# Biased attention and two MoE layers on one core: two relus of sets 8 to 10 and a rounding of k go to ScalarE, and the bias rows are loaded in two pieces

## The chip, the cores and the metric

One core of a Trainium2 chip runs the whole program. The metric is device time in microseconds (us) of one execution. Lower is better.

## The reference, cut to what matters

```python
scores = scale * q @ k.T                                  # (2, 8, 576, 576), scale = 1/8
rel = pos[:, None] - pos[None, :]                         # pos = 0 .. 575
psi_rel, psi_i = log1p(abs(rel)), log1p(max(pos[:, None], 1))
x = (psi_rel / psi_i)[..., None]
h = maximum(x @ w1 + b1, 0)                               # 32 hidden values for each (i, j)
bias = h @ w2                                             # 8 heads
attn = softmax(scores + bias)                             # + 1e-9 in the denominator
y = attn @ v                                              # (2, 576, 8 * 64) -> 1152 tokens of 512
hh = y @ w_in;  y = (hh * clip(hh + 3, 0, 6) / 6) @ w_out  # 512 -> 2048 -> 512
y = ((y @ w_a) * (y @ w_b)) @ w_out2                      # 512 -> 1536 -> 512
```

Everything is float32. The numerator of x depends only on the distance of two positions, and its denominator only on the row, so the bias of row i is a function of the distance alone.

## The kernel before, in words

**Bias.** The 576 rows are worked in 36 *sets* of 16 (`bias_relu(s)`, L183, and `bias_mm(s)`, L196). A set has four `ht` tiles of 128 partitions (4 rows times 32 hidden values), one for each j of 0 to 3, with the distance along the free axis. Each tile takes one relu with a scale per partition. `RELU = "VVVA"` (L87) puts j = 0 to 2 on VectorE (L192) and j = 3 on ScalarE (L194). Four matmuls with w2 give 16 rows times 8 heads, and `bias_out` (L220) copies them out of PSUM into a tile `E`, mirrored for negative distances: ScalarE does the right side (L227), VectorE the mirrored left side (L229). Both add a constant from `cst3`, a column that holds 8 times the value of the relu at zero for the partitions whose relu is the VectorE form max(scale * x, -b1), which leaves b1 out. One DMA (L243) writes `E`, skewed, into a scratch tensor in DRAM, and eight sets fill one scratch of 128 rows.

**Loading the bias back.** `bias_load(it, half)` (L248) reads a scratch into a tile `bias` of 128 partitions and 4 heads. Even heads take one DMA (576 columns), odd heads two (512 and 64 columns, since odd heads are rotated by 64). Three buffers hold `bias` tiles.

**Attention.** 36 steps n (L452) of one pair of heads of 128 rows each. Step n does the scores of pair n (L299, three products of rounded parts `KH`, `KL`, `qh`, `ql`), the softmax of pair n (L310 on VectorE adds the bias and takes the extreme, L314 on ScalarE is the exponential), the normalisation (L329 on GpSimd), the transposes of pair n-1 and the product with v of pair n-2. Between them it makes the bias of set g = n + 10. So the scratch of rows 128 to 255 is complete with set 15, in step 5; it is first used in step 8. The next two are complete with sets 23 and 31, in steps 13 and 21, and are first used in steps 16 and 24.

**The order of work** is the order in which the code issues it, per engine; nothing reorders it. SyncE (SP) issues nearly all DMAs, in order, and an issue that waits holds up those behind it. Each DMA also takes one of eight completion counters in turn, so that it waits until the DMA eight places ahead has landed.

**Places that the change touches.** Sets 0 to 9 are worked ahead of step 0 (L417 to L437). After the mm of set 7 come, in the code: the load of k's part 4, the rounding of k's part 1 (`k_hi(1, A)`, L430), the relus of sets 8 and 9, the rounding of q (`q_hi(0)`), the rounding of k's part 0 (`k_hi(0, V)`, L434), and on VectorE the rests `k_lo(0)`, `q_lo(0)`, `k_lo(1)` (L170, L150). The relus of set 10 come ahead of step 0 (L449), then `k_work(-1)` with two more roundings on ScalarE and two rests on VectorE. In a step n with g = 15, 23 or 31, L499 and L500 load the first two pairs of heads of the finished scratch, after the write of set g has been issued.

**MoE.** After step 35 TensorE runs the two MoE layers (L567, L773) from weights that ScalarE, VectorE and GpSimd split into parts.

Of the kernel before, what the change touches and what calls it, by code (L numbers as in the profile page):

```python
# [19 lines left out]
PITCH = 640  # L20
# [30 lines left out]
def kernel(ctx, tc, cons, qm, qt, kt, vm, vt, wm, out):  # L51
# [32 lines left out]
    negb = ph.tile([128, 1], F32, name="negb")  # L84
    cst4 = ph.tile([128, 1], F32, name="cst4")
    cst3 = ph.tile([128, 1], F32, name="cst3")
    RELU = "VVVA"  # L87


    idle = ph.tile([128, S], F32, tag="h", bufs=8, name="idle")  # L90
# [13 lines left out]
    V.tensor_scalar(scl, rtab, scalar1=w1c, scalar2=None, op0=ALU.mult)  # L104
    V.tensor_scalar(negb, b1c, scalar1=-1.0, scalar2=None, op0=ALU.mult)
    V.memset(cst3, 0.0)
    make_identity(nc, ident)
    warm = ph.tile([128, 1], F32, name="warm")
    G.memset(warm, 0.0)
# [56 lines left out]
    def k_hi(j, eng):  # L166
        (A.copy if eng is A else eng.tensor_copy)(KH[:, j, :], kr[j])
# [15 lines left out]
    def bias_relu(s, only=range(4)):  # L183

        i0, R, Dd = bias_geom(s)
        if s not in h_tiles:
            h_tiles[s] = [ph.tile([128, S], F32, tag="h", bufs=8, name="ht") for _ in range(4)]
        for j in only:
            ht = h_tiles[s][j]
            sc = scl[:, 4 * s + j : 4 * s + j + 1]  # L190
            if RELU[j] == "V":
                V.tensor_scalar(ht[:, :Dd], ltab[:, :Dd], scalar1=sc, scalar2=negb, op0=ALU.mult, op1=ALU.max)  # L192
            else:
                A.activation(ht[:, :Dd], ltab[:, :Dd], AF.Relu, bias=b1c, scale=sc)  # L194
# [25 lines left out]
    def bias_out(s, rev, banks, cuts):  # L220

        i0, R, Dd = bias_geom(s)
        E = ph.tile([128, S + 16], F32, tag="E", bufs=4, name="E")

        def leave(eng, dst, src):
            if eng is A:
                A.activation(dst, src, AF.Identity, bias=cst3[:, 0:1], scale=8.0)  # L227
            else:
                V.tensor_scalar(dst, src, scalar1=8.0, scalar2=cst3[:, 0:1], op0=ALU.mult, op1=ALU.add)  # L229

        for bp, d0, d1 in zip(banks, cuts, cuts[1:]):
            f1 = min(d1, S - i0)
            few = rev is A and Dd > 512
            if f1 > d0:
                leave(V if few else A, E[:, R + d0 : R + f1], bp[:, : f1 - d0])
            r0, r1 = max(d0, 1), min(d1, R + 1)
            if r1 > r0:
                dst = E[:, R - r1 + 1 : R - r0 + 1]
                dst = bass.AP(dst.tensor, dst.offset + (r1 - r0 - 1), [dst.ap[0], [-1, r1 - r0]])
                leave(V if few and d0 else rev, dst, bp[:, r0 - d0 : r1 - d0])  # L240
        it, sl = divmod(s, 8)
        scr = scratch[it]
        SP.dma_start(  # L243
            bass.AP(scr.tensor, scr.offset + PAD + 16 * sl * H * PITCH - 15, [[H * PITCH + 1, 16], [PITCH, H], [1, S + 15]]),
            E[:, : S + 15],
        )

    def bias_load(it, half, pairs=None):  # L248
        scr = scratch[it]
        if (it, half) not in bias_tiles:  # L250
            bias_tiles[it, half] = pa.tile([128, 4, S], F32, tag="bias", bufs=3, name="bias")
        bt = bias_tiles[it, half]
        p0, np_ = (0, 2) if pairs is None else (pairs, 1)
        for part in range(2 if it == 4 else 1):
            rows = 64 if it == 4 else 128

            for odd, j0, nj, at in ((0, 0, S, 0), (1, 0, 512, 64), (1, 512, 64, 0)):
                h0 = 2 * p0 + odd
                SP.dma_start(  # L259
                    bt[64 * part : 64 * part + rows, h0 : h0 + 2 * np_ - 1 : 2, at : at + nj],  # L260
                    bass.AP(
                        scr.tensor, scr.offset + PAD + (4 * half + h0) * PITCH + j0,
                        [[H * PITCH, rows], [2 * PITCH, np_], [1, nj]],
                    ),
                )
# [148 lines left out]
    bias_relu(0)  # L414
    V.tensor_scalar(cst4, bps0[:, 0:1], scalar1=8.0, scalar2=None, op0=ALU.mult)
    V.tensor_copy(cst3[0:96], cst4[0:96])
    for s in range(8 + LEAD):  # L417
        if s < 7:
            bias_relu(s + 1)
        elif s == 8:  # L420
            for half in range(2):
                for p in range(2):
                    bias_load(0, half, p)
        bias_mm(s, V)
        if s in (1, 3):
            load_k(2 + s // 2)
        elif s == 7:

            load_k(4)
            k_hi(1, A)  # L430
            for t in range(8, 8 + LEAD):
                bias_relu(t)
            q_hi(0)
            k_hi(0, V)  # L434
            k_lo(0, V)
            q_lo(0)
            k_lo(1, V)  # L437
# [14 lines left out]
    for n in range(NSTEP):  # L452
        g = n + 8 + LEAD
        if n % 4 == 2 and n // 4 + 2 <= 8:
            load_q(n // 4 + 2)
        qk_units(n)
        if n % 8 == 6 and n // 8 + 1 < 4:
            bias_load(n // 8 + 1, 1)
        if n >= 2:
# [32 lines left out]
        if g < NSET:  # L492
            if len(bps[0]) == 1:
                bias_out(g, A, *bps)
            if g == NSET - 1:
                bias_load(g // 8, 0)
            elif g % 8 == 7:

                bias_load(g // 8, 0, 0)  # L499
                bias_load(g // 8, 0, 1)  # L500
        if n == 29:
            bias_load(4, 1)
        denominators(n)
# [689 lines left out]
```

## Time and profile before

| what | value |
|---|---|
| time, median of 3 runs | 589.99 us (589.50 to 590.32) |
| the profiled execution | 589.66 us, of which the span is 587.8 us |
| busy in the span | PE 572.4, VectorE (DVE) 402.1, ScalarE (ACT) 333.7, GpSimd (POOL) 242.4 us |
| chain that ended last, by engine | PE 75%, DVE 11%, DMA 5%, POOL 3%, ACT 2% |
| chain, DMA parts | loads of the bias 3%, writes of the scratch 1% |

How to read it: the span runs from the first to the last instruction of the program, and what lies around it is 589.66 - 587.8 = 1.9 us. A busy PE is not PE at its peak, since matmuls are pipelined. From 166 us to the end the MoE layers keep PE busy; before that PE shares the pace with VectorE, and the questions of this change all lie in the first 130 us. Times below are us from the start of the span. In a timeline, "x3" is three instructions of one kind in a row, the second number is from the first's start to the last's end, and brackets hold the idle time of the engine ahead of it and what ended it. Instructions of one engine overlap by some 0.1 us at their ends.

### The profile page before, as it was taken

Reading aid. Unit: us, or ns where it says so; the run is one execution under the profiler, and the core shown is the slowest. Engines: PE = TensorE matmul, PEld = TensorE weight load, DVE = VectorE, ACT = ScalarE, POOL = GpSimd, SP = SyncE. Lnnn points to the kernel's source line nnn. Section 1 sums busy time; section 2 is a strip of 40 time slices with the busy share of each in tenths; the row PEclk is TensorE's granted clock in tenths of the full one; section 3 lists DMA queues with packets and bytes.
Section 4 is the critical chain, followed back from the end, with each engine's and each line's share of the span. In section 5 each row is a group of like instructions: output and inputs, shape, how many; then the busy total and the mean of one; then the engine's idle time right before and its main releaser. Section 6 shows DMA issues by size and latency. Waiting matters only on the chain.

```text
span 587.8 us, 13916 instructions
## 1 busy us (share of the span) xinstructions
PE 572.4 (97%) x5621; PEld 508.5 (87%) x5621; DVE 402.1 (68%) x807; ACT 333.7 (57%) x661; POOL 242.4 (41%) x255
## 2 busy tenths in 40 slices
PE   8799999997999999999999999999999999999997
PEld 5267777676789999999999999999889998899986
DVE  6899999998778725765764657956752649637252
ACT  6699999986767745723640654454455543345310
POOL 0067665667645312121121532464246834367200
PEclk9989999999999999999999999999999999999999
DMA  7794968386425542443342201011272122600012
GB/s 248 231 344 131 295 178 246 85 261 145 113 75 157 172 139 72 134 154 107 109 144 71 72 1 36 1 37 44 70 242 77 37 71 60 192 1 2 1 72 89
DMA packets 29072, 69.32 MB, mean 118 GB/s; under 512 B 5584, under 2 KB 5968, under 8 KB 29008
## 3 DMA queue, kind: packets, MB, share of 16 engines
q1 hardware_dynamic: 28864, 68.35, 37.8%
q8 instruction: 44, 0.72, 0.5%
q14 instruction: 20, 0.16, 0.1%
q10 hardware_dynamic: 144, 0.09, 0.1%
HBM read 55.17 MB, written 13.25 MB: 116 GB/s over the span
## 4 chain that ended last, share of the span: by engine, by line
PE 75%; DVE 11%; DMA 5%; POOL 3%; ACT 2%; issue 2%; SPq 1%; DVEq 0%; POOLq 0%; ACTq 0%
PE pair L567 44%; PE pair L773 21%; DMA bias<-scr 3%; PE bpw L214 2%; DVE ht L192 2%; PE sc L299 2%; POOL P L329 2%; DVE P L310 2%; PE pvb L391 2%; DMA scr<-E 1%; PE bps L214 1%; PE tp L335 1%; DVE PT L373 1%; SPq L259 1%; DVE tt L666 1%
## 5 line engine op out<-in xcount | busy, mean ns | idle before, releaser
L1015 POOL TENSOR_TENSOR slot<-wv,slot 128x512 fp32r<-128x512 f32 x86 | 118.7, 1384 | 221.0 <-ACT slot L1014 159.2
L567 PE MATMUL pair<-xx,slot 128*128 128x384 f32 x576 | 101.5, 335 | 0.0
L567 PEld LDWEIGHTS pair<-xx,slot 128*128 128x128 f32 x576 | 99.8, 188 | 0.3
L567 PE MATMUL pair<-gh,slot 128*128 128x384 f32 x384 | 98.5, 336 | 0.0
L773 PE MATMUL pair<-xx,slot 128*128 128x288 f32 x576 | 83.1, 296 | 0.3 <-DVE c L807 0.3
L773 PEld LDWEIGHTS pair<-xx,slot 128*128 128x128 f32 x576 | 78.6, 188 | 1.1 <-DVE c L807 0.6
L329 POOL TENSOR_SCALAR P<-P,st 128x576 f32<-128x576 f32 x72 | 55.9, 790 | 33.0 <-DVE st L324 17.1
L567 PEld LDWEIGHTS pair<-gh,slot 128*128 128x128 f32 x384 | 69.5, 188 | 0.0
L567 PE MATMUL pair<-slot,gh 128*128 128x512 f32 (+1 forms) x224 | 68.0, 386 | 0.0
L314 ACT ACTIVATE P<-P,st 128x576 f32<-128x576 f32 x72 | 55.8, 776 | 16.9 <-DVE st L310 16.1
L1014 ACT CAST slot<-wv 128x512 fp32r<-128x512 f32 x86 | 53.1, 622 | 20.9 <-PE pair L773 12.8
L773 PE MATMUL pair<-tt,slot 128*128 128x288 f32 x432 | 64.1, 297 | 0.7 <-ACT u L859 0.7
L567 PE MATMUL pair<-gl,slot 128*128 128x384 f32 x192 | 64.4, 336 | 0.0
L982 ACT ACTIVATE wv<-raw 128x512 f32<-128x512 f32 x63 | 42.4, 673 | 38.4 <-DMA raw<-in_wm_dram 25.3
L773 PEld LDWEIGHTS pair<-tt,slot 128*128 128x128 f32 x432 | 59.1, 188 | 2.3 <-ACT u L859 1.6
L592 ACT ACTIVATE t<-pair,three 128x384 f32<-128x384 f32 x48 | 28.0, 583 | 48.9 <-PE pair L567 48.9
L310 DVE CUSTOM_DVE_ANT_0 P<-sc,bias 128x576 f32<-128x576 f32 x72 | 51.6, 750 | 4.8 <-PE sc L299 2.5
L192 DVE TENSOR_SCALAR ht<-cs,scl,negb 128x576 f32<-128x576 f32 (+17 forms) x108 | 54.6, 542 | 0.0
L991 DVE TENSOR_SCALAR wm<-wv 128x512 uint32<-128x512 uint32 x59 | 40.5, 687 | 17.9 <-ACT wv L982 17.9
L593 DVE SCALAR_TENSOR_TENSOR u<-t,pair 128x384 f32<-128x384 f32 x48 | 26.6, 554 | 37.3 <-ACT t L592 37.3
L567 PEld LDWEIGHTS pair<-slot,gh 128*128 128x128 f32 x224 | 41.4, 188 | 8.7
L567 PE MATMUL pair<-slot,gl 128*128 128x512 f32 (+1 forms) x112 | 43.0, 384 | 0.0
(117 smaller groups left out, 931.3 us busy)
## 6 DMA issues: line engine op xcount, KB each, us to landing
raw<-in_wm_dram SPq DMA_DIRECT2D x68, 512.0 KB, 3.5
scr<-E SPq DMA_DIRECT2D x36, 295.5 KB, 4.1
bias<-scr SPq DMA_DIRECT2D x14, 288.0 KB, 4.2
bias<-scr SPq DMA_DIRECT2D x14, 256.0 KB, 4.7
kraw<-in_kt_dram SPq DMA_DIRECT2D x8, 288.0 KB, 4.7
qraw<-in_qm_dram SPq DMA_DIRECT2D x8, 256.0 KB, 4.7
VM<-in_vm_dram SPq DMA_DIRECT2D x2, 1024.0 KB, 8.2
out_dram<-part SPq DMA_DIRECT2D x7, 256.0 KB, 2.0
```

The lines of the kernel that those rows point to most:

```text
L192: V.tensor_scalar(ht[:, :Dd], ltab[:, :Dd], scalar1=sc, scalar2=negb, op0=ALU.mult, op1=ALU.max)
L310: V.tensor_tensor_reduce(out=Pu, in0=sc[:, :, 0:288], in1=bt, scale=-0.125, scalar=3.0e38, op0=ALU.add, op1=ALU.min, accum_out=st[:, u : u ...
L314: A.activation(P[:, u, :], P[:, u, :], AF.Exp, bias=st[:, u : u + 1], scale=-1.0, accum_out=st[:, 2 + u : 3 + u])
L329: G.tensor_scalar(P[:, u, :], P[:, u, :], scalar1=st[:, 2 + u : 3 + u], scalar2=1.0, op0=ALU.mult, op1=ALU.mult)
L567: T.matmul(ps_ap, l, r, start=(i == 0), stop=(i == len(prods) - 1))
L592: A.activation(t, hp, AF.Relu, bias=three[:, 0:1])
L593: V.scalar_tensor_tensor(out=u, in0=t, scalar=6.0, in1=hp, op0=ALU.min, op1=ALU.mult)
L773: T.matmul(pair[:, j, 0:TQ], l, r, start=start and i == 0, stop=i == 5, skip_group_check=not start)
L982: self.nc.scalar.activation(self.u[k], up, AF.Prelu, scale=2.0**-112, alpha=-(2.0**32))
L991: V.tensor_scalar(mid, ub, scalar1=3, scalar2=0x7FFFFFFF if k < NEARLY else 0xFFFFFFFF, op0=ALU.logical_shift_left, op1=ALU.bitwise_and)
L1014: nc.scalar.copy(s[:, 0, :], v)
L1015: nc.gpsimd.tensor_tensor(out=s[:, 1, :], in0=v, in1=s[:, 0, :].bitcast(F32), op=ALU.subtract)
```

## The change

- For sets 8, 9 and 10 the relus of j = 2 go to ScalarE too, so that each engine has two. Their constant is a new column `cst2`, which takes one memset and one copy more on VectorE at the start.
- `k_hi(0)` goes from VectorE to ScalarE, behind `q_hi(0)`.
- `bias_load` takes a range of rows. For the first scratch, the first pair of heads is loaded as rows 0 to 111 and rows 112 to 127, the load of k's part 4 goes behind the second pair, and the other half of the heads comes last.
- For the scratches that are finished with sets 15, 23 and 31, rows 0 to 111 of the first two pairs are loaded in the same step n, but ahead of the write of set g instead of behind it, and rows 112 to 127 after that write. Six loads become twelve.

```diff
--- before.py
+++ after.py
@@ -84,7 +84,8 @@
     negb = ph.tile([128, 1], F32, name="negb")
     cst4 = ph.tile([128, 1], F32, name="cst4")
     cst3 = ph.tile([128, 1], F32, name="cst3")
-    RELU = "VVVA"
+    cst2 = ph.tile([128, 1], F32, name="cst2")
+    two = range(8, 8 + LEAD + 1)
 
 
     idle = ph.tile([128, S], F32, tag="h", bufs=8, name="idle")
@@ -104,6 +105,7 @@
     V.tensor_scalar(scl, rtab, scalar1=w1c, scalar2=None, op0=ALU.mult)
     V.tensor_scalar(negb, b1c, scalar1=-1.0, scalar2=None, op0=ALU.mult)
     V.memset(cst3, 0.0)
+    V.memset(cst2, 0.0)
     make_identity(nc, ident)
     warm = ph.tile([128, 1], F32, name="warm")
     G.memset(warm, 0.0)
@@ -188,7 +190,7 @@
         for j in only:
             ht = h_tiles[s][j]
             sc = scl[:, 4 * s + j : 4 * s + j + 1]
-            if RELU[j] == "V":
+            if j < (2 if s in two else 3):
                 V.tensor_scalar(ht[:, :Dd], ltab[:, :Dd], scalar1=sc, scalar2=negb, op0=ALU.mult, op1=ALU.max)
             else:
                 A.activation(ht[:, :Dd], ltab[:, :Dd], AF.Relu, bias=b1c, scale=sc)
@@ -222,11 +224,13 @@
         i0, R, Dd = bias_geom(s)
         E = ph.tile([128, S + 16], F32, tag="E", bufs=4, name="E")
 
+        cst = cst2 if s in two else cst3
+
         def leave(eng, dst, src):
             if eng is A:
-                A.activation(dst, src, AF.Identity, bias=cst3[:, 0:1], scale=8.0)
+                A.activation(dst, src, AF.Identity, bias=cst[:, 0:1], scale=8.0)
             else:
-                V.tensor_scalar(dst, src, scalar1=8.0, scalar2=cst3[:, 0:1], op0=ALU.mult, op1=ALU.add)
+                V.tensor_scalar(dst, src, scalar1=8.0, scalar2=cst[:, 0:1], op0=ALU.mult, op1=ALU.add)
 
         for bp, d0, d1 in zip(banks, cuts, cuts[1:]):
             f1 = min(d1, S - i0)
@@ -245,21 +249,22 @@
             E[:, : S + 15],
         )
 
-    def bias_load(it, half, pairs=None):
+    def bias_load(it, half, pairs=None, r0=0, r1=128):
         scr = scratch[it]
         if (it, half) not in bias_tiles:
             bias_tiles[it, half] = pa.tile([128, 4, S], F32, tag="bias", bufs=3, name="bias")
         bt = bias_tiles[it, half]
         p0, np_ = (0, 2) if pairs is None else (pairs, 1)
         for part in range(2 if it == 4 else 1):
-            rows = 64 if it == 4 else 128
+            rows = 64 if it == 4 else r1 - r0
+            at0 = 64 * part + r0
 
             for odd, j0, nj, at in ((0, 0, S, 0), (1, 0, 512, 64), (1, 512, 64, 0)):
                 h0 = 2 * p0 + odd
                 SP.dma_start(
-                    bt[64 * part : 64 * part + rows, h0 : h0 + 2 * np_ - 1 : 2, at : at + nj],
+                    bt[at0 : at0 + rows, h0 : h0 + 2 * np_ - 1 : 2, at : at + nj],
                     bass.AP(
-                        scr.tensor, scr.offset + PAD + (4 * half + h0) * PITCH + j0,
+                        scr.tensor, scr.offset + PAD + (r0 * H + 4 * half + h0) * PITCH + j0,
                         [[H * PITCH, rows], [2 * PITCH, np_], [1, nj]],
                     ),
                 )
@@ -414,24 +419,27 @@
     bias_relu(0)
     V.tensor_scalar(cst4, bps0[:, 0:1], scalar1=8.0, scalar2=None, op0=ALU.mult)
     V.tensor_copy(cst3[0:96], cst4[0:96])
+    V.tensor_copy(cst2[0:64], cst4[0:64])
     for s in range(8 + LEAD):
         if s < 7:
             bias_relu(s + 1)
         elif s == 8:
-            for half in range(2):
-                for p in range(2):
-                    bias_load(0, half, p)
+            for r in ((0, 112), (112, 128)):
+                bias_load(0, 0, 0, *r)
+            bias_load(0, 0, 1)
+            load_k(4)
+            for p in range(2):
+                bias_load(0, 1, p)
         bias_mm(s, V)
         if s in (1, 3):
             load_k(2 + s // 2)
         elif s == 7:
 
-            load_k(4)
             k_hi(1, A)
             for t in range(8, 8 + LEAD):
                 bias_relu(t)
             q_hi(0)
-            k_hi(0, V)
+            k_hi(0, A)
             k_lo(0, V)
             q_lo(0)
             k_lo(1, V)
@@ -454,6 +462,9 @@
         if n % 4 == 2 and n // 4 + 2 <= 8:
             load_q(n // 4 + 2)
         qk_units(n)
+        if g < 32 and g % 8 == 7:
+            for p in range(2):
+                bias_load(g // 8, 0, p, 0, 112)
         if n % 8 == 6 and n // 8 + 1 < 4:
             bias_load(n // 8 + 1, 1)
         if n >= 2:
@@ -496,8 +507,8 @@
                 bias_load(g // 8, 0)
             elif g % 8 == 7:
 
-                bias_load(g // 8, 0, 0)
-                bias_load(g // 8, 0, 1)
+                for p in range(2):
+                    bias_load(g // 8, 0, p, 112, 128)
         if n == 29:
             bias_load(4, 1)
         denominators(n)
```

Where the instructions go, at the two places that matter. First VectorE between the `E` of set 7 and the first softmax (L310), before; `ht` are the relus (448, 432 and 416 columns: sets 8, 9 and 10), `KH` and `KL` the rounding of k and its rest, and 143 and 159 columns the mirrored `E` of sets 8 and 9:

```order
L229 TENSOR_SCALAR E<-bpw,cst_86 128x127
L192 TENSOR_SCALAR ht<-cs,scl,negb 128x448 x3
L192 TENSOR_SCALAR ht<-cs,scl,negb 128x432 x3
L167 CAST KH<-kraw 128x576
L170 TENSOR_TENSOR KL<-kraw,KH 128x576
L150 TENSOR_TENSOR ql<-qraw,qh 128x256
L170 TENSOR_TENSOR KL<-kraw,KH 128x576
L229 TENSOR_SCALAR E<-bpw,cst_86 128x143
L229 TENSOR_SCALAR E<-bpw,cst_86 128x159
L192 TENSOR_SCALAR ht<-cs,scl,negb 128x416 x3
L170 TENSOR_TENSOR KL<-kraw,KH 128x576 x2
L310 ISA P,st<-sc,bias 128x576
```

and with the change:

```order
L233 TENSOR_SCALAR E<-bpw,cst_86 128x127
L194 TENSOR_SCALAR ht<-cs,scl,negb 128x448 x2
L194 TENSOR_SCALAR ht<-cs,scl,negb 128x432 x2
L172 TENSOR_TENSOR KL<-kraw,KH 128x576
L152 TENSOR_TENSOR ql<-qraw,qh 128x256
L172 TENSOR_TENSOR KL<-kraw,KH 128x576
L233 TENSOR_SCALAR E<-bpw,cst_87 128x143
L233 TENSOR_SCALAR E<-bpw,cst_87 128x159
L194 TENSOR_SCALAR ht<-cs,scl,negb 128x416 x2
L172 TENSOR_TENSOR KL<-kraw,KH 128x576 x2
L315 ISA P,st<-sc,bias 128x576
```

VectorE has three relus and one rounding less, and its first `KL` reads a `KH` that another engine now makes. That engine is ScalarE, in the same stretch with the change:

```order
L231 ACTIVATE E<-bpw,cst_86 128x464
L169 CAST KH<-kraw 128x576
L196 ACTIVATE ht<-cs,scl 128x448 x2
L196 ACTIVATE ht<-cs,scl 128x432 x2
L147 CAST qh<-qraw 128x256
L169 CAST KH<-kraw 128x576
L231 ACTIVATE E<-bpw,cst_87 128x448
L231 ACTIVATE E<-bpw,cst_87 128x432
L196 ACTIVATE ht<-cs,scl 128x416 x2
L169 CAST KH<-kraw 128x576 x2
```

Before, the row of 448, that of 432 and that of 416 columns stood once each, and the second `KH` row was not there. So the `KH` of part 0 now stands behind four relus and the rounding of q.

The second place is SP around step 5, with the change; `scr_117` is the scratch of sets 8 to 15, and the four writes in the first two rows that name it are sets 12 to 14 and set 15:

```order
L247 DMA scr_117<-E 16x8x591 x3
L264 DMA bias<-scr_117 112x576
L264 DMA bias<-scr_117 112x512
L264 DMA bias<-scr_117 112x64
L264 DMA bias<-scr_117 112x576
L264 DMA bias<-scr_117 112x512
L264 DMA bias<-scr_117 112x64
L247 DMA scr_117<-E 16x8x591
L264 DMA bias<-scr_117 16x576
L264 DMA bias<-scr_117 16x512
L264 DMA bias<-scr_117 16x64
```

Three more loads of 16 rows, of the second pair, follow; then `qraw` and the other half of the heads. Before, the four writes stood together, and six loads of 128 rows came behind them.

## Rows read from the trace of the kernel before

**Rows 1.** 20 to 59: us; busy PE, PEld, DVE, ACT, POOL; clock; DMA share, GB/s.

```profile
20.00:59.00 39.00, 35.50 (x558) 23.40 (x562) 38.14 (x98) 34.26 (x79) 21.02 (x34) 0.91 0.74 233
```

**Rows 2.** Timeline of VectorE, steps 8, 8, 16 and 24: start, us, engine, line, shapes, idle.

```profile
59.60 0.76 DVE L310 CUSTOM_DVE_ANT_0 P<-sc,bias 128x576 f32<-128x576 f32 x1 [0.35 <-DMA bias<-scr]
...
60.52 0.76 DVE L310 CUSTOM_DVE_ANT_0 P<-sc,bias 128x576 f32<-128x576 f32 x1 [0.15 <-DMA bias<-scr]
...
91.10 0.76 DVE L310 CUSTOM_DVE_ANT_0 P<-sc,bias 128x576 f32<-128x576 f32 x1 [1.08 <-DMA bias<-scr]
...
123.07 0.75 DVE L310 CUSTOM_DVE_ANT_0 P<-sc,bias 128x576 f32<-128x576 f32 x1
```

**Rows 3.** Timeline of VectorE, 4 to 7 us.

```profile
4.50 0.06 DVE L106 MEMSET cst<- 128x1 f32 x1
...
6.25 0.15 DVE L416 COPY cst<-cst 96x1 f32<-96x1 f32 x1
```

**Rows 4.** Timeline of VectorE, 20 to 29 us.

```profile
20.57 2.60 DVE L192 TENSOR_SCALAR ht<-cs,scl,negb 128x448 f32<-128x448 f32 x6
23.08 0.45 DVE L167 CAST KH<-kraw 128x576 fp32r<-128x576 f32 x1
23.56 0.76 DVE L170 TENSOR_TENSOR KL<-kraw,KH 128x576 fp32r<-128x576 f32 x1
...
25.81 1.30 DVE L192 TENSOR_SCALAR ht<-cs,scl,negb 128x416 f32<-128x416 f32 x3
...
28.37 0.75 DVE L310 CUSTOM_DVE_ANT_0 P<-sc,bias 128x576 f32<-128x576 f32 x1
```

**Rows 5.** Timeline of ScalarE, 20 to 30 us.

```profile
20.16 0.66 ACT L167 CAST KH<-kraw 128x576 fp32r<-128x576 f32 x1
20.73 1.40 ACT L194 ACTIVATE ht<-cs,scl 128x448 f32<-128x448 f32 x2
22.03 0.39 ACT L145 CAST qh<-qraw 128x256 fp32r<-128x256 f32 x1
22.99 0.63 ACT L227 ACTIVATE E<-bpw,cst 128x448 f32<-128x448 f32 x1 [0.57 <-PE bpw L214]
...
25.35 1.24 ACT L167 CAST KH<-kraw 128x576 fp32r<-128x576 f32 x2
29.16 0.77 ACT L314 ACTIVATE P<-P,st 128x576 f32<-128x576 f32 x1 [2.57 <-DVE st L310]
```

**Rows 6.** SP's own timeline: writes of sets 14, 15; 22, 23; 30, 31; loads behind them.

```profile
48.29 4.62 SPq L243 DMA_DIRECT2D scr<-E  x2
55.53 3.59 SPq L259 DMA_DIRECT2D bias<-scr  x6
...
78.37 4.19 SPq L243 DMA_DIRECT2D scr<-E  x2
85.32 2.70 SPq L259 DMA_DIRECT2D bias<-scr  x6
...
110.07 4.50 SPq L243 DMA_DIRECT2D scr<-E  x2
117.28 2.72 SPq L259 DMA_DIRECT2D bias<-scr  x6
```

**Rows 7.** KB, us to landing of one write: set 14; set 15; 22, as 30.

```profile
scr<-E SPq DMA_DIRECT2D x1, 295.5 KB, 3.2
...
scr<-E SPq DMA_DIRECT2D x1, 295.5 KB, 3.0
...
scr<-E SPq DMA_DIRECT2D x1, 295.5 KB, 3.4
```

**Rows 8.** The same: a write at 91.20 behind nine loads; loads at 117.28, 55.53.

```profile
scr<-E SPq DMA_DIRECT2D x1, 295.5 KB, 7.3
...
bias<-scr SPq DMA_DIRECT2D x1, 288.0 KB, 2.8
...
bias<-scr SPq DMA_DIRECT2D x1, 288.0 KB, 3.9
```

## The prediction, made before the changed kernel had run

> **What bounds the kernel now.** I read the granted clock and span first, then the busy time by stretch, the chain of waits, and the timelines of the engines in the first 130 us, all that the change touches. In the stretch from 20 to 59 us VectorE is busy for 38.14 of 39.00 us [rows 1]: its order alone sets the pace there, and what it gains or loses ahead of the first softmax moves everything behind. Later PE and VectorE share the pace. The other bound is the handover of a finished scratch. VectorE's softmax (L310) waits for the bias in step 8, by 0.35 and 0.15 us, and in step 16 by 1.08 us; in step 24 it doesn't wait [rows 2]. The chain of waits also names the DMAs between 24 and 38 us. I don't follow it there, since VectorE has no gap in that stretch.
>
> From 166 us on PE runs the MoE layers without a break. They take the same work in the same order, so a shift at 130 us arrives at the end undiminished. I sum on the profiled execution's 589.66 us (span 587.8, 1.9 around it); the median of three runs is 589.99.
>
> **The start: the new column.** VectorE gains a memset and a copy, 0.06 and 0.15 us long [rows 3], which overlap their neighbours. VectorE feeds PE in that stretch. Bounds 0 and 0.21; I take **+0.1**.
>
> **Sets 8 to 10 and k's rounding.** VectorE loses a third of six relus, 2.60 / 3 = 0.87 us, the rounding of k's part 0, 0.45, and later a third of three relus, 1.30 / 3 = 0.43 [rows 4]: 1.75 us less work on the engine that sets the pace. ScalarE takes it over, and had idle time for it in the sum: 0.57 us ahead of the `E` of set 8, about as much ahead of set 9's, and 2.57 ahead of the first exponential [rows 5]. But look at the order. VectorE's next instruction, the rest of k's part 0, needs the rounding, which now ends ScalarE's new queue: relus of set 8 (two), of set 9 (two), q's rounding, k's rounding. Step by step: the first relu starts at 20.73, and one takes (22.03 - 20.73) / 2 = 0.65 [rows 5], so four end at 23.33. q's rounding takes 0.3 of its 0.39 before the next can start: 23.63. k's takes 0.66 to its end: **24.29**. VectorE is through with its four relus at 20.57 + 2.60 * 4 / 6 = 22.30 and then idles for 2.0 us. Its rest starts at 24.3 instead of 23.56 [rows 4], so it is 0.74 late. The one relu of set 10 that it no longer does gives 0.43 back, and the first softmax comes **0.3 us later**, at 28.7 instead of 28.37. The other waits on this way stay hidden: ScalarE's `E` of set 8 moves from 22.99 to 24.2, but VectorE's part of it waits behind the rests of k until 26; two relus of set 10 and k's two roundings then end near 27.8 and VectorE needs the first at 27.4. The 2.57 us of idle time cover that. Bounds: -0.3, if ScalarE's instructions overlap more, and +0.8, if PE, idle for longer ahead of step 0, also runs longer at the lower of its two clocks. The mean granted clock of 0.91 [rows 1] shows that a part of this stretch ran at 1.2 instead of 2.4 GHz.
>
> **The first scratch.** Its pair 0 is not what the first softmax waits for (VectorE has no gap), so its two pieces save nothing. SP gets three issues more, at 0.45 each, yet starts them a write earlier, when set 6 has landed. The load of k's part 4 goes behind nine loads; GpSimd rounds that part only in step 1, which covers it. Price 0, bounds 0 and 0.3.
>
> **The handover in steps 5, 13 and 21.** This is the main term. SP issues in order, and the six loads of rows 0 to 111 now stand *ahead* of the write of set g. They can't start until the write of set g-1 has landed. Step 5: the write of set 14 is issued at 48.29 [rows 6] and takes 3.2 us [rows 7]: 51.5. Six issues take 2.70 us [rows 6] (as at 85.32; those at 55.53 hold one more wait), so the write of set 15 is issued at 54.3. Before, it went at 48.29 + 4.62 - 0.52 = 52.39 [rows 6]. So it is **1.9 us late**. Alone it lands 3.0 later [rows 7]; but a megabyte of loads is ahead of it in the queue, and a write behind nine loads took 7.3 [rows 8]. The last of the six, issued at 53.8, lands about 3.2 later, and the write some 0.8 behind it: 57.8. Between 57.3 (alone) and that I take 57.8, as the queue moves in order. Now the 16-row loads. Their price is in no row. A 128-row load took 2.8 to 3.9 [rows 8]. Its 288 KB take at most 1.2 us of that, at the 233 GB/s of the stretch [rows 1], so the small one lies between 1.6 and 2.9; I take 2.4, nearer to the load that is in the rows. The second softmax of the step needs the third load, 2 * 0.45 later: 57.9 + 0.9 + 2.4 = 61.2, instead of the 60.52 at which it ran [rows 2]. **+0.7**, with 0 and +1.7 as the ends.
>
> The Trainium skill has a price for the small load: "DMA: Bandwidth & Descriptors", section "Anatomy of one DMA", puts one DMA at 2.0 us fixed plus its bytes over 436 GB/s. It is fitted on another path than SP's, and would give 2.1 us for 36 KB, so 60.9 and +0.4 in this step, a total 0.6 to 0.9 lower than mine, an estimate from that page. By its formula an eighth of the rows saves 0.6 us of 2.7.
>
> Step 13: the write of set 22 lands at 78.37 + 3.4 = 81.8 [rows 6, 7], six loads to 84.5, the write of set 23 then instead of at 82.04; it lands at about 88.1, and the third small load at 88.1 + 0.1 + 0.9 + 2.4 = 91.5, instead of 91.10 [rows 2]: **+0.4**. The wait of 1.08 us, which is all that the split could shorten, thus stays; the ends are -0.9 (a write that lands 3.0 after its issue, and small loads in 1.6) and +1.2. Step 21: 110.07 + 3.4 + 2.7 = 116.2, landed at 119.6, third load at 123.0 against 123.07 [rows 2]: **0**, up to +0.6.
>
> What queues behind: after twelve issues instead of six, q's next tile and the other half of the heads go out 2 us later (61.6 instead of 59.6). They are needed in step 10, at 67; they no longer stand behind a megabyte that is landing, which covers the delay.
>
> **Sum.** 0.1 + 0.3 + 0.7 + 0.4 + 0 = **+1.5 us**: 591.2 for the profiled execution, 591.5 against the median of 589.99. A measurement of this kernel can tell about 0.2% from no change, 1.2 us; the sum lies just above that.
>
> **Rivals.**
>
> *No change: small loads and write are quick.* The write isn't held by the loads' data and lands 3.0 after its issue, and the small loads take 2.2. Then step 8 gets its bias at 57.3 + 0.1 + 0.9 + 2.2 = 60.5 (0), step 16 at 84.6 + 3.0 + 3.2 = 90.8 (-0.3), and with 0.4 from the start the sum is +0.1: 590.1. For it: the writes in rows 7 took 3.0 to 3.4. Against it: they had an empty queue. The page's price of 2.1 us is of this case too. Chance 0.27.
>
> *Faster: VectorE's relief counts.* The mechanism is at ScalarE's queue ahead of k's rounding. If that rounding ends before 22.3, VectorE saves all of 1.75 us, and if the handovers then cost nothing, the time is 588.2. The point that decides is 23.85: by then the wait (22.3 to 23.85) and 0.43 less of set 10 cancel. For it: the relus are real work gone from the engine at 98% [rows 1]. Against it: the sum of rows 5 gives 24.29, and nothing in it may overlap further than the rows already show. A handover that gains step 16's whole wait, 1.08, against 0.4 lost at the start would come to 589.3 and isn't needed for this. Chance 0.16.
>
> *Slower by more: the half behind comes late.* SP's delay of 2 us goes on to the other half of the heads, which is needed in steps 10, 18 and 26. If these loads take as long as a write behind loads does, 7.3 [rows 8], they land at 68.9, and the softmax of step 10, due at 67 and now at 68.2, waits 0.7; the same in step 18. Time 593. Against it: the queue ahead of them is emptier. Chance 0.09.
>
> The forecast itself has 0.48.
>
> **How the numbers follow.** The forecast gives slower by over 0.2% in most of its cases (0.41 of 0.48), the late half 0.09: 0.50. No change takes 0.27 and the lower end of the forecast, 0.07: 0.34. Faster has 0.16. The range: the ends of the terms add up to about -1.2 and +4.8, and won't all come together. I take 589.0, which leaves out most of the faster case, and 593.4, beyond the late half.
>
> **What would show it.** Right: VectorE idle by some 2 us ahead of the first `KL`, waiting for ScalarE; the first softmax near 28.8; the write of set 15 behind six loads, issued some 2 us after its `E` is done; waits for the bias of about 1 us in steps 8 and 16. Wrong: no gap ahead of `KL`, a first softmax before 28.4, a 16-row load that lands under 2.0 us after its issue, or the softmax of step 16 without a wait.

## The result: slower by 0.9%, and the profile after

| | before | with the change |
|---|---|---|
| time, median | 589.55 us | 594.06 us |
| ratio, with its 95% interval | | 1.0092 (1.0071 to 1.0112) |
| the profiled execution | 589.66, span 587.8 | 593.82, span 592.0 |

The medians stand 4.5 us apart, where 1.5 were forecast; the ratio puts the cost at 5.4 us (4.2 to 6.6). Below, each run has its median and, in brackets, its ratio to the kernel before with the interval; where the two disagree the ratio counts. The two profiled executions stand 4.2 us apart in their spans. The start of the softmax (L310 before, L315 now) shows where, worked out from VectorE's timelines:

| softmax | before | after | shift | of it new |
|---|---|---|---|---|
| step 0 | 28.37 | 27.45 | -0.9 | |
| step 7 | 55.46 | 55.04 | -0.4 | +0.5 |
| step 8, second | 60.52 | 62.10 | +1.6 | +2.0 |
| step 10 | 66.97 | 70.08 | +3.1 | +1.5 |
| step 15 | 85.33 | 88.43 | +3.1 | 0 |
| step 16, second | 91.10 | 95.22 | +4.1 | +1.0 |
| step 24, first | 122.41 | 126.62 | +4.2 | +0.1 |
| step 35 | 165.58 | 169.78 | +4.2 | 0 |

The +0.5 of steps 1 to 3 is half of a lead that this execution had from its start (below), lost in a stretch at the lower clock that both profiles show. First VectorE from the relus of set 8 to the first softmax, which answers to [rows 4]:

```profile
19.31 1.75 DVE L194 TENSOR_SCALAR ht<-cs,scl,negb 128x448 f32<-128x448 f32 x4
23.06 0.76 DVE L172 TENSOR_TENSOR KL<-kraw,KH 128x576 fp32r<-128x576 f32 x1 [2.00 <-ACT KH L169]
...
27.45 0.75 DVE L315 CUSTOM_DVE_ANT_0 P<-sc,bias 128x576 f32<-128x576 f32 x1
```

and ScalarE in the same stretch, as in [rows 5]:

```profile
19.46 2.69 ACT L196 ACTIVATE ht<-cs,scl 128x448 f32<-128x448 f32 x4
22.06 0.40 ACT L147 CAST qh<-qraw 128x256 fp32r<-128x256 f32 x1
22.35 0.67 ACT L169 CAST KH<-kraw 128x576 fp32r<-128x576 f32 x1
```

Look at the distance between two rows of one engine rather than at the clock time. From the first relu of set 8 to the first softmax it was 28.37 - 20.57 = 7.80 us [rows 4] and is 8.14. That the relus began 1.26 us sooner in this execution is no merit of the change: `steps_only` and `write_pair0` below start with the same instructions as the kernel before, and have 20.55 and 19.31 there.

Now SP's own timeline around steps 5 and 13, as in [rows 6]:

```profile
47.78 0.52 SPq L247 DMA_DIRECT2D scr<-E  x1
51.09 2.68 SPq L264 DMA_DIRECT2D bias<-scr  x6
53.81 0.52 SPq L247 DMA_DIRECT2D scr<-E  x1
58.76 2.96 SPq L264 DMA_DIRECT2D bias<-scr  x6
...
88.15 0.52 SPq L247 DMA_DIRECT2D scr<-E  x1
92.56 2.62 SPq L264 DMA_DIRECT2D bias<-scr  x6
```

The time to landing (last number) of the write issued at 53.81, of that at 88.15, and of the first 16-row load, which answers to [rows 7, 8]:

```profile
scr<-E SPq DMA_DIRECT2D x1, 295.5 KB, 4.9
...
scr<-E SPq DMA_DIRECT2D x1, 295.5 KB, 4.4
...
bias<-scr SPq DMA_DIRECT2D x1, 36.0 KB, 1.7
```

Behind six loads the write takes 4.9 and 4.4 us, where it took 3.0 to 3.4 alone. The second six issues hang on it: 58.76 is 53.81 + 4.9. VectorE then waits in steps 8 and 16, not in step 24, as in [rows 2]:

```profile
60.56 0.76 DVE L315 CUSTOM_DVE_ANT_0 P<-sc,bias 128x576 f32<-128x576 f32 x1 [1.74 <-issue]
...
62.10 0.76 DVE L315 CUSTOM_DVE_ANT_0 P<-sc,bias 128x576 f32<-128x576 f32 x1 [0.78 <-PE sc L340]
...
94.54 0.76 DVE L315 CUSTOM_DVE_ANT_0 P<-sc,bias 128x576 f32<-128x576 f32 x1 [2.08 <-issue]
...
126.62 0.73 DVE L315 CUSTOM_DVE_ANT_0 P<-sc,bias 128x576 f32<-128x576 f32 x1
```

The brackets name "issue" and PE, though the 16-row loads land at 60.44 and 61.98 (58.76 + 1.7, and the third's), 0.12 us ahead of these starts: a wait for several semaphores is put down to one of them only. Last, the stretches of steps 8 and 9, with the columns of [rows 1], before and after:

```profile
58.00:64.50 6.50, 6.12 (x134) 4.80 (x137) 5.99 (x17) 5.99 (x15) 3.49 (x7) 1.00 0.91 286
64.50:68.00 3.50, 3.50 (x83) 2.62 (x75) 3.50 (x12) 3.50 (x10) 2.56 (x6) 1.00 1.00 338
```

```profile
58.00:64.50 6.50, 4.32 (x86) 3.08 (x83) 3.98 (x12) 4.07 (x10) 2.05 (x4) 1.00 0.34 90
64.50:68.00 3.50, 3.50 (x53) 2.42 (x51) 2.56 (x8) 2.50 (x7) 2.73 (x4) 0.51 0.98 333
```

PE was busy 4.32 instead of 6.12 us in the late step, and in the next 3.5 us its granted clock is 0.51, the lower level (1.2 GHz): 53 matmuls in the time of 83. That is the 1.5 us between steps 8 and 10 in this profile, which no term of the forecast had.

### The profile page after: what moved, and what is told of

It reads as the page before. It is cut to its first block, busy times and chain, and to the rows that moved or that the text cites. A ratio compares the mean times of both kernels' runs of the same rounds, so it can differ in the third digit from the quotient of the medians.

```text
span 592.0 us, 13948 instructions
## 1 busy us (share of the span) xinstructions
PE 573.1 (97%) x5621; PEld 508.4 (86%) x5621; DVE 400.5 (68%) x805; ACT 336.2 (57%) x665; POOL 242.1 (41%) x255
## 4 chain that ended last, share of the span: by engine, by line
PE 80%; DVE 6%; ACT 6%; DMA 4%; issue 2%; POOL 2%; SPq 0%; DVEq 0%; POOLq 0%; ACTq 0%
PE pair L578 44%; PE pair L784 21%; PE sc L304 4%; PE pvb L396 3%; DMA scr<-E 2%; PE bpw L216 2%; PE bps L216 2%; PE tp L340 2%; ACT P L319 2%; POOL P L334 2%; ACT PT L376 1%; PE sc L340 1%; PE pvb L392 1%; DVE P L315 1%; ACT E L231 1%
## 5 line engine op out<-in xcount | busy, mean ns | idle before, releaser
L315 DVE CUSTOM_DVE_ANT_0 P<-sc,bias 128x576 f32<-128x576 f32 x72 | 51.5, 751 | 8.2 <-issue 3.8
```

Of the source, the lines that this page charges most:

```text
L315: V.tensor_tensor_reduce(out=Pu, in0=sc[:, :, 0:288], in1=bt, scale=-0.125, scalar=3.0e38, op0=ALU.add, op1=ALU.min, accum_out=st[:, u : u ...
```

## The experiments

Theory A: the loss comes from the order on SP, the write of set g behind six loads, and from what follows from the late bias. Rival B: the start carries it, by ScalarE's longer queue. Rival C: more and smaller DMAs cost in themselves.

### Each part alone

`relus_only` has the relus, `cst2` and `k_hi(0, A)`, with the loads as before. `steps_only` has the split loads of steps 5, 13 and 21 alone, `first_only` those of the first scratch.

> Only the relus of sets 8 to 10, cst2 and the rounding of k's part 0 go to ScalarE; all bias loads as before. Theory A (the order on SP: the write of set g stands behind six loads, the bias comes late in steps 8 and 16, and PE, starved there, falls to its lower clock): this part costs its 0.35 us at the start and nothing else, 589.9 us against 589.55 (589.4 to 590.4), and the softmax of steps 8 and 16 waits as in the kernel before. Rival B (the start carries the loss: ScalarE's longer queue ahead of k's rounding): 592 or more. Rival C (more and smaller DMAs cost by themselves): as theory A.

> Only the loads of steps 5, 13 and 21 are split and moved as in the change (rows 0 to 111 ahead of the write of set g, rows 112 to 127 behind it). Theory A: nearly the whole loss, 592.5 to 594.5 us, with the write of set 15 landing 4.5 to 5 us after its issue, a wait for the bias of over 1 us in step 8, and a drop of the granted clock to 0.5 behind it. Rival B: 590 to 591. Rival C: as theory A.

> Only the loads of the first scratch are in the change's order (pair 0 in two pieces, k's part 4 behind the second pair). Theory A: nothing waits for these loads, 589.2 to 590.0 us. Rival B (the start carries the loss, here through the loads of the first scratch): 591 or more. Rival C: three DMAs more cost some tenths of a us.

Measured: 589.94 us (ratio 1.0007, 0.9991 to 1.0023), **594.62** (1.0082, 1.0056 to 1.0107) and 589.24 (0.9985, 0.9971 to 1.0000). B falls. In the profile of the relus alone the stretch from relu to softmax is 8.15 us (20.45 to 28.60), as with the whole change. The steps alone make nearly the whole loss (4.8 us, 3.3 to 6.3; the median is 0.1 above the range I had put), and in their trace the write of set 15 lands 4.2 us after its issue and that of set 23 4.6. The expected drop of the clock stands behind step 16 there, not behind step 8.

### The order of the twelve loads

`write_first` is the whole change with the write issued first:

```diff
-        if g < 32 and g % 8 == 7:
-            for p in range(2):
-                bias_load(g // 8, 0, p, 0, 112)
...
-                for p in range(2):
-                    bias_load(g // 8, 0, p, 112, 128)
+                for r in ((0, 112), (112, 128)):
+                    for p in range(2):
+                        bias_load(g // 8, 0, p, *r)
```

> The whole change but one thing: in steps 5, 13 and 21 the six loads of rows 0 to 111 are issued behind the write of set g, directly ahead of the six loads of rows 112 to 127. The DMAs are the same in number and size. Theory A (the order is the cost): the write lands some 3.0 to 3.4 us after its issue, steps 8 and 16 wait less than 1 us more than before, no drop of the clock behind step 8: 589.5 to 591.0 us. Rival C (the number and size of the DMAs is the cost, not their order): 592.5 or more. Rival B: 592 or more.

Measured: **592.96** (1.0057, 1.0037 to 1.0076), a miss for A. SP, then VectorE in step 8:

```profile
51.24 0.52 SPq L247 DMA_DIRECT2D scr<-E  x1
51.98 6.38 SPq L264 DMA_DIRECT2D bias<-scr  x12
```

```profile
60.74 0.76 DVE L315 CUSTOM_DVE_ANT_0 P<-sc,bias 128x576 f32<-128x576 f32 x1 [2.50 <-DMA bias<-scr]
```

The write is early and lands in 3.4 us, and still step 8 waits 2.50. Pair 0's small loads are the seventh to ninth issue; the first goes out at 54.9 and lands 5.7 us later, behind the data of the six large ones. This profile is of the slowest of the eight runs, and a part of the wait isn't the place in the queue: from 59.0 to 60.0 the queue is busy on 7.0% of the 16 DMA engines, about one of them (more on that below). So either C holds, or A has to be put wider (A2): what counts is everything that stands ahead of pair 0's small loads in SP's queue, write or load. `by_pair` turns the two loops round: the same twelve loads, pair 0's first.

> The whole change, but in steps 5, 13 and 21 the write of set g goes first and the twelve loads follow pair by pair: pair 0's rows 0 to 111, pair 0's rows 112 to 127, then pair 1's. The run with the same twelve loads and pair 0's small ones behind all six large ones had 592.96. If the place of the small loads was the cost, pair 0 is complete after six loads, in time for steps 8 and 16, and the time is 588.6 to 590.0 us. If number and size of the loads were the cost: 592 to 593.5.

Measured: 590.49 (1.0017, 1.0005 to 1.0029), 2.5 us less by order alone, with intervals that don't touch, and the wait of step 8 shrinks to 0.27:

```profile
58.33 0.76 DVE L315 CUSTOM_DVE_ANT_0 P<-sc,bias 128x576 f32<-128x576 f32 x1 [0.27 <-DMA bias<-scr]
```

The place of the loads is the main cost. Number and size can explain no more than what is left, 1.0 us above the kernel before (0.3 to 1.7), in which the start of the change is contained; the median is half a us above the range I had put. Two more variants have the start of the kernel before. In `write_pair0` the write goes first, then pair 0 in two pieces, then pair 1 whole; in `pair0_ahead` pair 0's rows 0 to 111 go ahead of the write, the rest behind it.

> The start is as in the kernel before; in steps 5, 13 and 21 the write of set g goes out first, then only pair 0 is split (rows 0 to 111, then 112 to 127), then pair 1 whole: nine loads, and the three small ones stand behind three others and not behind six. Theory A2 (the loss is what stands ahead of the small loads of pair 0 in SP's queue, whether that is the write held up by six loads or the six loads themselves): the small loads land near 58.3 in step 8 and 89.0 in step 16, before the softmax wants them, so the waits of 0.5 and 1.08 us of the kernel before go too: 588.0 to 589.2 us, and no drop of the clock behind step 8 or 16. Rival C (each load more costs in itself, or loads of 112 and 16 rows are slow): 590.5 or more.

> The start is as in the kernel before; in steps 5, 13 and 21 only pair 0's three loads of rows 0 to 111 go ahead of the write of set g; behind it come pair 0's three small loads and pair 1 whole. Theory A2: three loads take half as long to issue as six, so the write of set 15 is late by some 0.5 us and that of set 23 by 1.1, and they land some 4 us after their issue; the small loads land near 58.5 and 89.7, still in time: 588.3 to 589.8 us. Theory A as first put (any load ahead of the write costs): halfway between before and the run with the split steps alone, 591 to 592.5. Rival C: 590.5 or more.

Measured: **588.46** (0.9983, 0.9967 to 0.9998) and 590.04 (1.0003, 0.9991 to 1.0015). With no load ahead of the write 1.0 us is gained by the ratio (0.1 to 1.9), with three nothing is left of it, and with the six of `steps_only`, which also splits pair 1, 4.8 are lost. Three were a little dearer than I expected, and C is out as the main cause: nine loads are faster than six. In both traces the waits of steps 8 and 16 are gone (0.16 us is left in step 16 of `pair0_ahead`), but new ones of up to 0.7 us stand in steps 10 and 18, for the other half of the heads.

### The start: order or sum of ScalarE's work

`roundings_first` is `relus_only` (three relus moved, one of each set, so that ScalarE has six in all) with `k_hi(0, A)`, `q_hi(0)` ahead of `k_hi(1, A)` and the relus. `one_less` leaves the relus of sets 8 and 9 as before; set 10 alone has two and two, behind the roundings of k's parts 2 and 3:

```diff
+    two = range(8 + LEAD, 8 + LEAD + 1)
...
-            k_hi(0, V)
+            k_hi(0, A)
...
+    k_hi(2, A)
+    k_hi(3, A)
     bias_relu(8 + LEAD)
```

> As the run with the relus alone (all six relus of j = 2 gone to ScalarE, loads as before), but ScalarE rounds k's part 0 and q ahead of k's part 1 and of the relus. If only k's place in the queue ate VectorE's relief, the wait of 2.0 us ahead of the first rest of k goes and the first softmax comes 1.2 to 1.7 us sooner: 588.0 to 588.7 us. If ScalarE's sum of work is the bound (it now has four relus, two bias copies, two more relus and two more roundings ahead of VectorE's last two rests of k), VectorE's wait only moves behind, to those last rests, and the first softmax comes at the earliest 0.2 us later than in the kernel before: 589.7 to 590.5 us. I hold the second.

> The loads are as in the kernel before. The rounding of k's part 0 goes to ScalarE behind that of q, as in the change, but the relus of sets 8 and 9 stay as they were, and only set 10 has two on each engine; the roundings of k's parts 2 and 3 go ahead of set 10's relus on ScalarE. If the wait behind four relus in ScalarE's queue is what ate VectorE's relief, k's rounding now ends at 23.0, before VectorE wants it at 23.1, and the first softmax comes 0.4 to 0.9 us sooner: 588.6 to 589.2 us. If VectorE's work ahead of the first softmax doesn't set the pace: 589.4 to 589.9, as the kernel before.

Measured: 590.17 (1.0016, 1.0004 to 1.0027) and **588.56** (0.9986, 0.9972 to 0.9999). VectorE with the roundings first:

```profile
19.45 1.76 DVE L194 TENSOR_SCALAR ht<-cs,scl,negb 128x448 f32<-128x448 f32 x4
...
23.73 0.37 DVE L233 TENSOR_SCALAR E<-bpw,cst 128x143 f32<-128x143 f32 x1 [0.85 <-ACT E L231]
24.83 0.38 DVE L233 TENSOR_SCALAR E<-bpw,cst 128x159 f32<-128x159 f32 x1 [0.74 <-ACT E L231]
...
26.64 1.43 DVE L172 TENSOR_TENSOR KL<-kraw,KH 128x576 fp32r<-128x576 f32 x2 [0.61 <-ACT KH L169]
27.98 0.75 DVE L315 CUSTOM_DVE_ANT_0 P<-sc,bias 128x576 f32<-128x576 f32 x1
```

The one wait of 2.0 us has become three of 0.85 + 0.74 + 0.61 = 2.2, and the stretch is 27.98 - 19.45 = 8.53 us. So it is the sum of ScalarE's work that counts, not the place of k's rounding in it. With one relu and one rounding moved, instead of three and one:

```profile
19.21 2.59 DVE L194 TENSOR_SCALAR ht<-cs,scl,negb 128x448 f32<-128x448 f32 x6
21.72 0.75 DVE L172 TENSOR_TENSOR KL<-kraw,KH 128x576 fp32r<-128x576 f32 x1
...
26.11 0.76 DVE L315 CUSTOM_DVE_ANT_0 P<-sc,bias 128x576 f32<-128x576 f32 x1
```

6.90 us and no wait: 0.9 less than before, the 0.45 of k's rounding and the 0.43 of set 10's relu. VectorE's relief was real, and the change moved more than ScalarE could take in time. The time bears it out less sharply: 0.8 us by the ratio (0.1 to 1.7).

### TensorE's clock

Does the drop behind step 8 follow from PE's idle time in it? `filled` is the whole change with matmuls that nobody reads, at the two places of steps 8 and 16 where PE waits; `filled_less` has 4 calls instead of 14 (two instructions each), `filled_8` those in step 8 alone.

```diff
+    def fill(n, bps):
+        if n in (8, 16):
+            for _ in range(14):
+                T.matmul(bps[0][0][:, 448:512], ident, ident[:, 0:64], start=True, stop=True)
```

> The whole change, and in steps 8 and 16 TensorE also does 28 small matmuls (128x64) into columns of the bias bank that nobody reads, 14 ahead of each of the two gaps in which it waits for the late softmax. If the drop of the granted clock behind step 8 follows from TensorE's idle time there, it goes, and with it 1.4 us or more: 591.5 to 593.0 us, and the profile shows no clock below full from 58 to 100 us. Rival D (the clock drops as the run will have it, whatever TensorE does in steps 8 and 16): 594.0 or, with the added matmuls, 594.5, and a drop in the profile as often as before.

> The whole change, and 8 instead of 28 small matmuls at each of the two gaps of TensorE in steps 8 and 16 (a run of 28 took 3.34 us, so 8 take 0.95, about the length of the gap). If the drops of the granted clock follow from the idle time in these gaps, the runs have a mean clock of 0.996 or more (0.9925 over the twelve runs of the change) and the time is 591.5 to 593.2 us. Rival D (the drops have nothing to do with these gaps): mean clock 0.993, 594 to 595 us.

> The whole change, with two runs of 8 small matmuls in TensorE's two gaps of step 8, none in step 16. If the drop behind step 8 follows from TensorE's idle time there, most runs are without it: 592.0 to 593.3 us and a mean clock of 0.994 or more (a drop behind step 16 may stay). If it doesn't: 594 to 595 us at 0.9925, as the change itself.

Measured: 600.50 (1.0185, 1.0167 to 1.0202), 598.53 (1.0171, 1.0144 to 1.0198) and 600.93 (1.0184, 1.0152 to 1.0216). All three times miss. But the forecast of `filled` for the clock came true: between 58 and 67 us PE is busy for 9.00 of 9.00 us, and its granted clock is 1.00 from 55 to 110 us. Steps 8 and 9 of `filled_less`, then of `filled_8`:

```profile
58.00:64.50 6.50, 6.50 (x107) 5.16 (x107) 4.33 (x14) 4.42 (x11) 2.00 (x4) 1.00 0.42 114
64.50:68.00 3.50, 3.50 (x83) 2.81 (x86) 3.50 (x10) 3.42 (x10) 2.88 (x5) 1.00 1.04 332
```

```profile
58.00:64.50 6.50, 6.00 (x95) 4.67 (x94) 3.28 (x10) 3.36 (x9) 1.95 (x4) 1.00 0.19 38
64.50:68.00 3.50, 3.11 (x39) 2.74 (x43) 2.86 (x10) 2.78 (x7) 2.24 (x5) 0.56 0.95 305
```

With the same matmuls in step 8 the clock held in one profile, with PE busy for 6.50 of 6.50 us, and fell in the other, with 6.00.

Does the change bring these drops? Of the sixteen profiles of this case five have a clock below 1.00 between 55 and 110 us: the change, `steps_only`, `write_first`, `filled_less` and `filled_8`. In each a softmax waits 1.9 us or more in step 8 or 16. In the others none waits longer than 1.42 us, but for `filled`, where PE was kept busy. The mean clock of whole runs says the same: 0.9925 over twelve of the change and 0.9927 over twelve of `steps_only`, against 0.9964 over 31 of the kernel before, run beside `steps_only`; 0.9952 for `relus_only`, 0.9975 for `first_only`, 0.9976 for `filled`. So the change does bring the drops: they come with a late softmax, and where PE had no gap (`filled`, and step 8 of `filled_less`) there was none. The 0.9964 - 0.9925 = 0.0039 of some 590 us are 2.3 us, an estimate of what the clock has in the loss over all runs, if PE sets the pace there. Why it falls behind one late step and not behind another **stays open**: behind the change's step 16, which waits 2.08 us, it held.

The times missed for other reasons. In `filled` the added matmuls were in the way: a run of 28 takes 3.34 us, there are four, and VectorE waits 3.43 and 3.36 us for the scores of steps 9 and 17. In the other two, transfers landed later. In `filled_8` (its profile is of the slowest run, 605.75 us) the write of set 23, issued at 89.00, took 6.7 us. The DMAs while it was under way, from 89.0 to 92.4 and from 92.6 to 95.1 (packets, MB, share of 16 engines):

```profile
q1 hardware_dynamic: 579, 0.79, 79.0%
q8 instruction: 1, 0.02, 1.6%
```

```profile
DMA packets 31, 0.05 MB, mean 20 GB/s; under 512 B 10, under 2 KB 10, under 8 KB 31
...
q1 hardware_dynamic: 31, 0.05, 6.6%
```

For the last 2.5 us in which it moves anything the queue is busy on 6.6% of 16 engines: about as much as one of them (6.25%), with 31 packets. The write counts as landed at 95.7, behind the last of these. In step 5 of the change the tail is there too: from 57.3 to 58.7, with the write issued at 53.81 under way, the queue moves 10 packets, 4.0%.

```profile
DMA packets 10, 0.02 MB, mean 14 GB/s; under 512 B 2, under 2 KB 2, under 8 KB 10
...
q1 hardware_dynamic: 10, 0.02, 4.0%
```

All ten lie ahead of 58.2, and up to the landing nothing moves, as for 0.3 us ahead of the landing of the same write before. So about 0.9 of the 4.9 us belong to one late engine. In both cases one load of instructions (the row q8, 16 KB in one packet) ran beside the transfers shortly before. That it held that engine up fits, but it is not shown: 15 such loads run from 37 to 129 us, so that one is seldom far away, the views don't name the engine, and no run took the load away.

### Both gains together

`both` is `one_less` with the loads of `write_pair0`. `both_pairs` also loads the other half of the heads pair by pair in steps 6, 14 and 22:

```diff
-            bias_load(n // 8 + 1, 1)
+            for p in range(2):
+                bias_load(n // 8 + 1, 1, p)
```

> The two parts that gained alone, together: k's part 0 rounded on ScalarE, set 10 with two relus on each engine, k's parts 2 and 3 rounded ahead of them; and pair 0 split behind the write in steps 5, 13 and 21. If they add up: 1.2 + 1.3 = 2.5 us, 587.1 to 587.6. If the other half of the heads, which lands by the clock of SP's queue and not by that of the softmax, takes what was gained (as the wait of 0.6 to 0.7 us in step 18 of both traces suggests), 587.8 to 588.6. I hold the second.

> As the run before in this list, and in steps 6, 14 and 22 the other half of the heads is loaded pair by pair, six loads instead of three. Pair 2 then has half the bytes ahead of it and should land over 1 us sooner, so the wait of steps 10 and 18 goes: 0.5 to 0.8 us less than the run without it. If the three more issues hold up the writes behind them instead: the same or up to 0.5 us more.

Measured: 587.85 (0.9969, 0.9955 to 0.9983) and **586.20** (0.9954, 0.9942 to 0.9965). By the medians the parts gained 1.2 and 1.3 us alone and 1.6 together, but by the ratios it is 0.8 and 1.0 alone and 1.8 together, so that the times don't show that anything is lost. The trace of `both`, its slowest run of twelve, does wait in steps 10 and 18 for the other half:

```profile
64.74 0.76 DVE L315 CUSTOM_DVE_ANT_0 P<-sc,bias 128x576 f32<-128x576 f32 x1 [0.67 <-DMA bias<-scr]
66.24 0.76 DVE L315 CUSTOM_DVE_ANT_0 P<-sc,bias 128x576 f32<-128x576 f32 x1 [0.73 <-DMA bias<-scr]
...
97.60 0.76 DVE L315 CUSTOM_DVE_ANT_0 P<-sc,bias 128x576 f32<-128x576 f32 x1 [1.42 <-DMA bias<-scr]
```

By pairs these waits are gone (this profile is the fastest of six runs). I had put 0.5 to 0.8 us less than `both`; the medians give 1.65, the ratios 0.9, and the two intervals overlap. The kernel is 2.7 us faster than the one before by the ratio (2.1 to 3.4), which is clear of noise:

```profile
63.99 0.73 DVE L315 CUSTOM_DVE_ANT_0 P<-sc,bias 128x576 f32<-128x576 f32 x1
64.65 0.75 DVE L315 CUSTOM_DVE_ANT_0 P<-sc,bias 128x576 f32<-128x576 f32 x1
...
94.61 0.76 DVE L315 CUSTOM_DVE_ANT_0 P<-sc,bias 128x576 f32<-128x576 f32 x1
```

## Why the prediction was wrong

- **Start, +0.1 and +0.3: right.** k's rounding was to end 3.72 us after the first relu of set 8 on VectorE (24.29 - 20.57); it ended 3.71 after it (22.35 + 0.67 - 19.31). The idle time is 2.00, the stretch 0.34 longer, and `relus_only` measures +0.4, with an interval from -0.5 to +1.4. The 0.1 for the new column no run shows by itself.
- **First scratch, 0: right.** `first_only` is at most 1.7 us faster (its interval) and not slower.
- **Step 5/8, +0.7: the step that failed.** The mechanism was right, the write behind six loads and the small loads behind the write, and so was its issue (54.3 forecast, 53.81 with this execution's lead of 0.42). "Between 57.3 (alone) and that I take 57.8" was wrong: with the lead added back it landed at 58.74 + 0.42 = 59.2, 1.4 late. I took the landing of the last load plus the write's share of the data, as if sixteen engines ended together; the late engine has about 0.9 of the 1.4 in this profile. From issue to landing the forecast had 3.5 us; it took 4.9 here and 4.2 in `steps_only`. The nearest row I had for a write with a full queue ahead was 7.3 us [rows 8], and I kept it out of that term's bounds. The 16-row loads were quicker than taken, 1.7 to 2.0 us instead of 2.4, which gave back 0.4 at the third; that one was issued 1.2 instead of 0.9 behind the first. Together +2.0 instead of +0.7.
- **The term that was missing.** Nothing priced what a late softmax does to PE. It stood idle in step 8, and the stretch behind ran at the lower clock: +1.5 in this profile, and by the clocks of all runs some 2.3 us of the loss (the estimate above). I had allowed for the clock at the start alone.
- **Step 13/16, +0.4:** measured +1.0, by the same term (4.4 us to landing instead of some 3.6). **Step 21/24, 0:** right by luck. The write took 4.3 us instead of 3.4 here too, and the small loads, 1.7 instead of 2.4, made up for most of it; 0.2 us were left (the first small load landed at 126.40, the softmax ran at 126.62). `steps_only` does wait there, 0.39 us.
- **Rivals.** "No change" falls with the write's 4.9 us, although its small loads of 2.2 us were nearer than mine. "Faster" fails at the point named: on the time of the profile before, k's rounding came 0.4 behind 23.85. (By the prediction's own rows the two cancel at 23.56 + 0.43 = 23.99; it came behind that too.) `one_less` shows what that rival would have needed. "The half behind comes late" is hardly in the change (0.27 us in step 18), where the steps ahead were already late; it shows in the traces of `write_pair0` and `both`, where they no longer were.
- **Range.** Its upper end, 593.4, left the term of step 8 its bound of +1.7 and no clock. The trace of before held a warning: with an empty queue ahead of both writes, step 16 still waited 1.08 us.

On the 16-row loads the price of the Trainium skill ("DMA: Bandwidth & Descriptors", "Anatomy of one DMA"), 2.1 us as an estimate by its formula, which is fitted on another path than SP's, was nearer than mine: with nothing ahead of them the trace shows 1.7 to 2.0. The same page, section "Why a DMA increments its semaphore by 16 and not by 1", says that a DMA runs on up to 16 engines that finish independently, and that only the full count means all data has landed. This case's trace agrees: in `filled_8` a queue at 6.6% of 16 engines holds a write for 2.5 us. By this rule the landing of a write behind other data is set by its slowest engine, and a mean rate, as I took it, is the earliest it can be.

## What to carry to other kernels

In a queue that is worked in order, splitting a load only helps if the small part that ends the wait stands near the front: here the kernel with the same twelve loads takes 594.06, 592.96 or 590.49 us by their order. Price a transfer behind others by the slowest row with a full queue, not by adding mean rates. And move work off a busy engine piece by piece: one relu and one rounding gained 0.8 us where three relus and the rounding gained nothing (+0.4, not clear of noise).

## What had not been expected of the hardware

- A transfer's end can hang on about one of sixteen engines for 0.9 to 2.5 us (above). Landing times also change with an edit elsewhere: in `filled_less` the write of set 22, which nothing of the edit touches, took 5.7 us instead of 3.8. The row q8 counts 44 loads of instructions in 0.72 MB, 16 KB each. The Trainium skill ("Runtime: NRT & Kernel Launch", "Instruction fetch mechanics") says that instructions come in 16 KiB blocks over a DMA queue of their own, at a cost that is mostly hidden; the block size agrees, and whether the cost was hidden here no run settles.
- A matmul of 128x64 with a 128x128 stationary operand took 3.34 / 28 = 0.12 us when 28 ran in a row, and 1.10 / 8 = 0.14 us when eight did.
